# A state-space scan and a windowed attention in one kernel: output rows in pairs, last sums added on VectorE, K's weights in halves, another order of issue

## The chip, the cores and the metric

The kernel runs on one core of a Trainium2 chip. The metric is the device time of one execution in microseconds (us), the median of several runs. The engines named below are TensorE (PE; its weight loads are listed as PEld), VectorE (DVE), ScalarE (ACT), GpSimd (POOL) and SyncE (SP), which here does nothing but issue transfers; "SPq" is its queue. PSUM is the memory that TensorE writes its sums to; ScalarE and VectorE copy ("evict") them to SBUF, the core's working memory.

## The reference

There are two independent parts. Each takes its own input x of 2048 tokens by 448 values, in bf16. Their results are put side by side, 448 columns each, in one output of 2048 x 896.

```python
# Part A: state-space layer, 448 complex states
Lam_bar = exp(dt * Lam);  B_bar = ((Lam_bar - 1) / Lam)[:, None] * Bmat
Bu = einsum("bld,pd->blp", x, B_bar)
h[t] = Lam_bar * h[t-1] + Bu[t]                    # over 2048 tokens
y = 2 * real(einsum("blp,dp->bld", h, Cmat)) + x * Dskip
# Part B: attention of 16 heads of 28, each query sees the 8 keys s, s-2, .., s-14
q, k, v = split(x @ wqkv)
logits = einsum("bhsd,bhswd->bhsw", q, kg) * 28**-0.5   # kg, vg: the 8 keys and values of each query
attn = softmax(logits, masked where s - 2w < 0)
o = einsum("bhsw,bhswd->bhsd", attn, vg);  out = o @ wo
```

## The kernel before, in words

**Layout.** Token s = 16p + j stands in partition p (0 to 127) as token j (0 to 15). So what the text calls "token j" is 128 tokens of the sequence, one in each partition. Matrix products want the features on the partitions, so x is transposed: for tokens 12 to 15 by TensorE from a plain load (`pt_x`, L426), for the others by transposing DMAs (L361). 448 features are one block of 64 and three of 128; the block of 64 is handled by pairs of matmuls in the two halves of the array's rows (L483), the three others by L476.

**Part B.** The weights of K and then of Q are loaded by a helper `wload` (L338 for the three blocks of 128 features, L340 for the 64 that are left). Projections go to `qk_ps` (L476, L483, L509 for the last columns) and are evicted, some by ScalarE (L214, L216), some by VectorE (L218, L220; the line is a helper's). VectorE multiplies queries and keys (`prods`, L649 to L655), TensorE sums over the head's 28 values (L666), VectorE, ScalarE and TensorE make the softmax (L695 to L735). The values are evicted to `vd`; the rows that a partition needs from its neighbour are copied by DMA (the "halo", L775 and L776, four times). Then VectorE forms attention times values in four groups of four tokens, 3, 2, 1 and 0: per group four multiplications (L817) and the sums (L820). The windowed sum comes in two halves of 1792 columns, which for groups 3, 2 and 1 are added by L829; a transposing DMA (L857) and the `wo` matmuls (L885, L893) follow. In group 0, the last, nothing adds the halves: L832 adds the last product in two parts (tokens 0 and 1, then 2 and 3), and TensorE transposes by products with the identity (`pt_o`, L869), eight a token, two of which go to the same columns, so that PSUM adds the halves. ScalarE copies `pt_o` to SBUF (L874), four `wo` matmuls (L900) and an eviction (L214) follow. Token 2's eviction is shared by ScalarE (256 columns) and VectorE (192).

**Part A.** POOL prepares parameters, VectorE makes powers of Lam_bar (`pw`, L1182). For each of seven groups of states the input matmuls (L1232, L1241) fill PSUM, and a chain of matmuls and small ScalarE copies (L1256 to L1333) does the scan: within 16 tokens of a partition, then over the 128 partitions, and back. The carried state stands in a tile S of its own for the last token, so the step that hands the carry on takes a matmul of 128 columns and one of 384 (L1307, L1308). The output of a token is seven matmuls of 448 columns (L1434), with x * Dskip as further matmuls (L1430) or, for tokens 12 to 15, by VectorE (multiplied by L1411, added in the eviction by L1446).

**Outputs.** Each token's 448 columns of either part go out in one transfer of 128 x 448: L1449 for part A, L910 for part B, 32 in all. Staging rows come from rings: 8 rows for part A (`ya`), 4 for part B (`yb`). A row is taken at the eviction and is free again when its transfer has landed.

**Order.** All work is registered as units (an engine, a cost, predecessors, rings). Where the list `ORDER` has as many entries as there are units (687 before, 693 after), it is the order of issue as it stands; an entry above 1000 puts an eviction on the other of its two engines. Each engine works its list in order and waits at the head of it. Nearly all transfers are issued by SP, one after another, so a transfer whose data is not ready holds back all behind it. At the start TensorE runs products of zeros: `WARM` of them at once, and `FILL` of them behind each of the two batches of transposes.

Of the kernel before, what the change touches and what calls it, by code (L numbers as in the profile page):

```python
# [10 lines left out]
ALU = mybir.AluOpType  # L11
# [14 lines left out]
W = 8  # L26
# [6 lines left out]
QW = 2 + NCH  # L33
LV2 = ((1, 2, 3), (4, 8, 12), (16, 32, 48))
KPOW = sorted({1, 2, 4, 8, 12, 16} | {32 * k for ks in LV2 for k in ks})
# [4 lines left out]
WARM = 4  # L40
FILL = (1, 3)
# [4 lines left out]
YG = ((3,), (7,), (11,), (1, 5), (9,), (0, 4), (8,), (2, 6), (10,), (12, 13), (14,), (15,))  # L46
YSPLIT = 8
ORDER = [
# [156 lines left out]
class Ctx:  # L205
# [83 lines left out]
    def warm(self):  # L289
# [5 lines left out]
        nc.vector.memset(z, 0.0)  # L295
        box = {}
# [10 lines left out]
    def late_tile(self):  # L307
        if self.late is None:
            self.late = self.rc
            self.ya_v = self.late[:, 8448:8448 + 3584].rearrange("p (r d) -> p r d", r=8)  # L310
            self.yb_v = self.late[:, 12032:12032 + 1792].rearrange("p (r d) -> p r d", r=4)
            self.ya_ring, self.yb_ring, self.ya_row = Ring(8), Ring(4), {}
        return self.late


class PartB:
# [7 lines left out]
    def loads(self):  # L324
# [11 lines left out]
        def wload(c0, c1):  # L336
            w = self.wqk[:, :, c0:c1] if c0 < 2 * D else self.wv
            nc.sync.dma_start(w[:, 1:4], self.B_wqkv[DT:D, c0:c1].rearrange("(k p) c -> p k c", p=NCH))  # L338
            for rows in ((slice(DT, NCH),) if c0 < 2 * D else (slice(0, DT), slice(DT, NCH))):
                nc.sync.dma_start(w[rows, 0], self.B_wqkv[0:DT, c0:c1])  # L340
        self.wload = wload
# [4 lines left out]
        wload(D, 2 * D)  # L346
        self.u_x3 = [P.add("ACTQ", 0.0, lambda: None, lat=t) for t in (3.45, 3.95)]
        self.u_w["K"] = P.add("ACTQ", 0.0, lambda: None, lat=6.2)

    def loads_more(self):  # L350
# [16 lines left out]
        u0 = self.u0 = P.add("SP", 2.35, lambda: None, lat=0.0)  # L367
        self.u_w["Q"] = P.add("SP", 1.0, lambda: self.wload(0, D), [u0], -1, lat=4.4)
# [8 lines left out]
    def load_v(self, deps):  # L377
        self.u_w[2] = self.plan.add("SP", 1.2, lambda: self.wload(2 * D, 3 * D), deps, 0.5, lat=3.5)
# [32 lines left out]
    def prep(self, u_warm):  # L411
# [6 lines left out]
        def xpose(j):  # L418
            box = {}

            def tr():
                pt = box["pt"] = self.psum.tile([NCH, 2, KT, NCH], bf16, name="pt_x", tag="s")
                for n in range(2):
# [3 lines left out]
            u = P.add("PE", 0.9, tr, [self.u_x3[(j - 12) // 2]], -8.5, acq="s")  # L427
# [24 lines left out]
        def banks(b, r, tiles, boxes, prio, rfirst):  # L452
# [5 lines left out]
            for kind, kt in tiles:  # L458
                wd.append(self.u_wm if kind == "M" else self.u_w[kind])
# [1111 lines left out]
```

## Time and profile before

| what | value |
|---|---|
| device time, median of 3 runs | 139.18 us (138.98 to 139.67) |
| device time of the profiled execution | 140.44 us |
| its span from first to last instruction | 138.7 us |
| busy: PE, DVE, ACT, POOL | 131.6, 123.8, 90.0, 17.7 us |
| matmuls; instructions of DVE, ACT | 1078; 136, 202 |
| DMA | 39582 packets, 16.05 MB |
| output transfers | 32 of 112 KB, median 1.8 us from issue to landing |

Between the span and the device time of the profiled execution lie 1.7 us, and the profiled execution is 1.3 us above the median. A row of the groups reads: line, engine, operation, what it writes and reads with sizes, count | busy us, mean ns of one | idle time of the engine just ahead of these instructions and what ended it. In the timeline a row is: start, length, engine, line, operation, and in brackets the idle time ahead and what ended it. A row of the windows names a stretch of the span and then its length, the busy time and count of PE, PEld, DVE, ACT and POOL, the granted clock of TensorE, the share of the DMA engines that is busy and GB/s.

### The profile page before, as it was taken

What the parts mean: (1) busy time and instruction counts of PE and PEld (TensorE: products, weight loads), DVE (VectorE), ACT (ScalarE), POOL (GpSimd) and SP (SyncE); (2) the same over time, 40 slices, a digit from 0 to 9 for tenths busy, and PEclk for the clock granted to TensorE, in tenths of its full rate; (3) what the DMA queues carried; (4) which work ended last, traced back from release to release, by engine and by line L of the source; (5) the groups of instructions that cost most, each with busy time, mean ns of one, the idle gap of its engine ahead of it and who ended that gap; (6) DMA issues with size and microseconds to landing.
All of it is one profiled execution on the core that took longest, in us unless ns stands there. A gap on an engine that the chain in (4) does not pass through costs nothing.

```text
span 138.7 us, 2854 instructions
## 1 busy us (share of the span) xinstructions
PE 131.6 (95%) x1078; PEld 68.5 (49%) x1085; DVE 123.8 (89%) x136; ACT 90.0 (65%) x202; POOL 17.7 (13%) x69
## 2 busy tenths in 40 slices
PE   5999999999999999999999999999999999988990
PEld 1634435444555554756435564545655554534640
DVE  2268999899999999999999999999999999999820
ACT  3464589997563967776685998987637070722671
POOL 7489820028000000000000000000000000000000
PEclk9999999999999999999999999999999999999999
DMA  4979943645653349735898019000000827965774
GB/s 128 266 128 213 173 87 63 160 101 116 80 111 74 82 84 145 140 81 150 230 185 195 0 25 112 0 0 2 5 0 0 183 82 43 213 211 155 234 233 139
DMA packets 39582, 16.05 MB, mean 116 GB/s; under 512 B 31573, under 2 KB 38932, under 8 KB 39569
## 3 DMA queue, kind: packets, MB, share of 16 engines
q1 hardware_dynamic: 39506, 15.87, 54.0%
q8 instruction: 8, 0.13, 0.4%
q14 instruction: 5, 0.04, 0.1%
q10 hardware_dynamic: 63, 0.01, 0.0%
HBM read 4.32 MB, written 3.67 MB: 58 GB/s over the span
## 4 chain that ended last, share of the span: by engine, by line
DVE 35%; PE 31%; SPq 15%; issue 7%; DMA 6%; ACT 3%; DVEq 0%; ACTq 0%
DVE rb L820 13%; DVE prods L817 11%; SPq L361 8%; PE v_ps L762 7%; DVE rb L817 4%; PE qk_ps L476 4%; DMA out_dram<-qk 3%; PE logits L666 3%; PE y_ps L1434 3%; DMA rb<-in_B_x_dram 3%; DVE pw L1182 2%; DVE rb L829 2%; PE wo_ps L900 2%; PE scb L1232 2%; PE scp L1232 2%
## 5 line engine op out<-in xcount | busy, mean ns | idle before, releaser
L817 DVE TENSOR_TENSOR prods<-attn,vd 128x3584 bf16<-128x3584 bf16 x12 | 24.1, 2019 | 0.0
L820 DVE TENSOR_TENSOR rb<-rb,prods 128x3584 bf16<-128x3584 bf16 x11 | 22.2, 2021 | 0.1
L651 DVE TENSOR_TENSOR prods<-qk 128x3072 bf16<-128x3072 bf16 (+1 forms) x15 | 19.1, 1327 | 0.0
L214 ACT CAST qk<-wo_ps 128x448 bf16<-128x448 f32 (+1 forms) x16 | 8.3, 527 | 12.2 <-PE wo_ps L893 7.7
L1434 PE MATMUL y_ps<-Ccat,qk 128*128 128x448 bf16 x60 | 15.1, 352 | 0.1
L476 PE MATMUL qk_ps<-rb 128*128 128x512 bf16 x60 | 14.4, 379 | 0.0
L1434 PE MATMUL y_ps<-Ccat,h 128*128 128x448 bf16 x45 | 11.0, 352 | 0.9 <-ACT qk L214 0.9
L214 ACT CAST vd<-v_ps 128x448 bf16<-128x448 f32 x15 | 7.4, 539 | 5.8 <-PE v_ps L762 4.5
L1232 PE MATMUL scb<-xaT_sb,Bcat 128*128 128x512 bf16 x42 | 10.9, 380 | 0.0
L1232 PEld LDWEIGHTS <-Bcat 128*128 128x128 bf16 x84 | 7.6, 100 | 6.6 <-issue 0.4
L1284 ACT CAST ubuf<-scb 128x64 bf16<-128x64 f32 x35 | 7.1, 218 | 5.6 <-PE scb L1291 3.5
L762 PE MATMUL v_ps<-rb 128*128 128x448 bf16 x48 | 9.9, 353 | 0.0
L655 DVE TENSOR_TENSOR prods<-qk 128x768 bf16<-128x768 bf16 (+3 forms) x18 | 9.1, 569 | 0.3 <-ACT qk L214 0.2
L216 ACT ACTIVATE qk<-qk_ps 64x512 bf16<-64x512 f32 (+1 forms) x15 | 8.9, 599 | 0.6 <-PE qk_ps L509 0.3
L476 PEld LDWEIGHTS <-rb 128*128 128x128 bf16 x60 | 5.6, 98 | 7.1 <-DMA rb<-in_B_wqkv_dram 0.5
L1434 PEld LDWEIGHTS <-qk 128*128 128x128 bf16 x60 | 5.9, 98 | 5.3
L817 DVE TENSOR_TENSOR rb<-attn,vd 128x3584 bf16<-128x3584 bf16 x4 | 8.1, 2022 | 0.1
L893 PE MATMUL wo_ps<-wo_p,rb 128*128 128x448 bf16 x36 | 8.1, 354 | 0.0
L1182 DVE TENSOR_TENSOR pw<-Dm,spair 128x1920 bf16<-128x1920 bf16 x7 | 8.1, 1153 | 0.0
L214 ACT CAST qk<-qk_ps 128x512 bf16<-128x512 f32 (+2 forms) x11 | 6.3, 585 | 2.6 <-PE qk_ps L483 1.1
L1232 PE MATMUL scp<-xaT_sb,Bcat 128*128 128x512 bf16 x30 | 7.8, 380 | 0.0
L666 PE MATMUL logits<-prods,Zsel 128*32 128x256 bf16 x192 | 7.4, 274 | 0.0
(199 smaller groups left out, 261.9 us busy)
## 6 DMA issues: line engine op xcount, KB each, us to landing
out_dram<-qk SPq DMA_DIRECT2D x32, 112.0 KB, 1.8
vd<-vd SPq DMA_DIRECT2D x3, 392.0 KB, 4.7
rb<-in_B_wqkv_dram SPq DMA_DIRECT2D x3, 336.0 KB, 5.0
qk<-in_A_x_dram SPq DMA_DIRECT2D x1, 448.0 KB
ra<-in_A_B_re_dram SPq DMA_DIRECT2D x1, 392.0 KB, 4.3
ra<-in_A_B_im_dram SPq DMA_DIRECT2D x1, 392.0 KB, 5.9
rb<-in_A_C_re_dram SPq DMA_DIRECT2D x4, 98.0 KB, 2.9
rb<-in_A_C_im_dram SPq DMA_DIRECT2D x4, 98.0 KB, 2.8
```

The lines of the kernel that those rows point to most:

```text
L214: nc.scalar.copy(out, in_)
L361: nc.sync.dma_start(self.xT[:, j], bass.AP(x.tensor, x.offset + j * D - DT, [[T * D, NCH], [1, KT * NCH]]), transpose=True)
L476: nc.tensor.matmul(out(n), lhsT=w(n, full, k), rhs=self.xT[:, j:j + 4, k, :], start=(not rfirst and k == 1), stop=(rfirst and k == KT - 1) ...
L651: V.tensor_tensor(out.rearrange("p i j k q -> p i (j k) q"), qq.unsqueeze(1).to_broadcast([NCH, 2, 4 * nk, NCH]), bass.AP(kk.tensor, kk.of ...
L655: V.tensor_tensor(jk(out[:, i, a:e]), qq, kk, op=ALU.mult)
L666: nc.tensor.matmul(lg[32 * i:32 * i + 32, 2 * tp:2 * tp + 2, :], lhsT=cx.Z[:, kt, zs], rhs=pr[:, :, i, kt, :], start=(new and kt == 0), st ...
L762: nc.tensor.matmul(box["ps"][:].rearrange("p h d -> p (h d)"), lhsT=self.xT[:, j, k, :], rhs=self.wv[:, k, :], start=False, stop=(k == KT ...
L817: V.tensor_tensor(tmp[i].rearrange("p (j d h) -> p j d h", j=8, d=DH), aa, self.vd[:, o:o + 8], op=ALU.mult)
L820: V.tensor_tensor(acc, acc, tmp[i], op=ALU.add)
L1182: V.tensor_tensor(t[:], self.o["Dm"][:].rearrange("p (a b) -> p a b", b=2).unsqueeze(1).to_broadcast([NCH, 2 * NPW, 32, 2]), self.sp[:, m ...
L1232: mt(box[i], lhsT=self.Bcat[:, k, m, :], rhs=self.xk(slice(i, None, 4), k), start=(i % 2 == 0 and k == 0), stop=False, **kw)
L1434: nc.tensor.matmul(ps, lhsT=h, rhs=self.Ccat[:, m, :], start=(m == 0 and not skip), stop=(m == NM - 1), skip_group_check=True)
```

## The change

Line numbers here are those of the kernel after, unless said otherwise.

- **Output pairs.** Part A's 16 tokens leave in 8 transfers of 128 x 2 x 448 (L1492, the list `OUTP`), groups 3, 2 and 1 of part B in 6 (L939); the four tokens of group 0 still go one by one (L942). The ring `yb` has 6 rows. Rows are taken two at a time by units of their own, and freed together. Token 2's last eviction is one instruction.
- **Last sums.** With `MERGE`, VectorE adds the two halves of group 0 behind each of its two last additions (L855, 128 x 896), and `pt_o` takes four products a token in place of eight.
- **K's weights in halves.** K's columns come as 256 and 192 (L346). The 64 rows that are left, for K and Q, are one transfer that ScalarE issues. K's first projections (tokens 12 to 15) run as halves of two tokens; the copy of the 64 rows for the second half of the array is made per 128 columns. Tokens 14 and 15 have transposes and copies of their own.
- **Zero products.** `WARM` 4 to 5, `FILL` (1, 3) to (1, 2): the sum is eight in both.
- **Scan.** The tile S is gone; the states of the last block lie with gaps of four columns, so that the carry is one matmul of 512 columns (two places a group, 14 matmuls fewer, as many columns).
- **Order.** `ORDER` is another list. On TensorE, the seven output matmuls of one token of part A move behind the first eight `pt_o` products at the end. On SP, the second transpose of attention sums stands ahead of the last halo copy (L796, L797). On VectorE there is one eviction of `qk_ps` more (15 for 14), two copies of 64 x 512 more and one eviction to `vd` fewer.

```diff
-WARM = 4
-FILL = (1, 3)
+MERGE = 1
+WARM = 5
+FILL = (1, 2)
+OUTP = ((1, 5), (2, 6), (0, 4), (12, 13), (7, 11), (8, 9), (3, 10), (14, 15))
 ORDER = [
...
-        wload(D, 2 * D)
+        for c0, c1 in ((D, D + 256), (D + 256, 2 * D)):
+            nc.sync.dma_start(self.wqk[:, 1:4, c0:c1], self.B_wqkv[DT:D, c0:c1].rearrange("(k p) c -> p k c", p=NCH))
...
+        nc.scalar.dma_start(self.wqk[DT:NCH, 0], self.B_wqkv[0:DT, 0:2 * D])
+        nc.scalar.copy(cx.first[:, 1:2], cx.first[:, 0:1])
...
+            elif j == 12 and tiles[0][0] == "K":
+                us = []
+                for a in (0, 2):
+                    for n in range(2):
+                        us.append(P.add("PE", pe(3, 256), lambda n=n, a=a: f(n, a, a + 2), x[a:a + 2] + wd + us[-1:], prio, acq=None if a else "s"))
+                u = P.add("PE", pe(1, 512), rr, [us[-1]] + dup, prio, mode="r")
...
                         a, t = (v.rearrange("p (y j c) -> p y j c", y=2, j=4)[:, :, 2 * part:2 * part + 2] for v in (acc, tmp[3]))
                         V.tensor_tensor(a, a, t, op=ALU.add)
+                        if MERGE:
+                            V.tensor_tensor(a[:, 0], a[:, 0], a[:, 1], op=ALU.add)
...
-                    for y in range(2):
+                    for y in range(2 - MERGE):
                         c = y * n1 + a + kt * NCH
                         nc.tensor.matmul(pt[:, kt, :], lhsT=self.rb2[:, c:c + NCH], rhs=cx.ident[:],
-                                         start=(kt == 0 and y == 0), stop=(y == 1), skip_group_check=True)
+                                         start=(kt == 0 and y == 0), stop=(y == 1 - MERGE), skip_group_check=True)
...
-            def out(j=j, jb=jb):
-                nc.sync.dma_start(self.out_b[:, j, :], cx.yb_v[:, jb["y"]])
+            def out(j=j, jb=jb, g=g):
+                if g:
+                    a, b = jb["mate"]["y"], jb["y"]
+                    nc.sync.dma_start(self.out_b[:, j - 1:j + 1, :], cx.yb_v[:, a:b + 1:b - a])
+                    cx.yb_ring.put(a)
...
-            if j == 2:
-                es = [P.add("ACT", act(D - 192), lambda f=ev2: f(c1=D - 192), [u], pr, acq="yb")]
-                es.append(P.add("DVE", vec(192), lambda f=ev2: f(c0=D - 192, eng="DVE"), [u, *es], pr, rel="s"))
...
-            def carry(out, lt, Sc, hv):
-                mt(out[:, 0:NCH], lhsT=lt, rhs=Sc, start=False, stop=True, **kw)
-                mt(out[:, NCH:512], lhsT=lt, rhs=hv[:, 3, 0:384], start=False, stop=True, **kw)
...
+            def s6(box=box, L=L, hget=hget):
+                mt(box[0].rearrange("p (g c) -> p g c", g=4), lhsT=L(1), rhs=hget()[1][:, :, 2:2 + NCH],
+                   start=False, stop=True, **kw)
...
-            def out(j):
-                nc.sync.dma_start(self.out_a[:, j, :], cx.ya_v[:, cx.ya_row[j]])
-                cx.ya_ring.put(cx.ya_row[j])
+            def out(a, b):
+                nc.sync.dma_start(self.out_a[:, a:b + 1:b - a, :], cx.ya_v[:, rows[a]:rows[b] + 1:rows[b] - rows[a]])
+                cx.ya_ring.put(rows[a])
+                cx.ya_ring.put(rows[b])
```

More of the change, by code (lines that the diff above doesn't have):

```diff
@@ L295, in warm @@
         nc.vector.memset(z, 0.0)
+        self.first = self.pool.tile([NCH, 2], f32, name="first")
+        nc.vector.memset(self.first[:, 0:1], 0.0)
         box = {}
@@ L377, in load_v, with go @@
     def load_v(self, deps):
-        self.u_w[2] = self.plan.add("SP", 1.2, lambda: self.wload(2 * D, 3 * D), deps, 0.5, lat=3.5)
+        nc = self.nc
+        def go():
+            v = self.B_wqkv[:, 2 * D:3 * D]
+            nc.sync.dma_start(self.wv[:, 1:4], v[DT:D].rearrange("(k p) c -> p k c", p=NCH))
+            for rows in (slice(0, DT), slice(DT, NCH)):
+                nc.sync.dma_start(self.wv[rows, 0], v[0:DT])
+        self.u_w[2] = self.plan.add("SP", 1.2, go, deps, 0.5, lat=3.5)
     def alloc(self):
@@ L416, in prep, with xpose @@
         sc = DH ** -0.5
-        def xpose(j):
+        def xpose(j, nt):
             box = {}
             def tr():
-                pt = box["pt"] = self.psum.tile([NCH, 2, KT, NCH], bf16, name="pt_x", tag="s")
-                for n in range(2):
+                pt = box["pt"] = self.psum.tile([NCH, nt, KT, NCH], bf16, name="pt_x", tag="s")
+                for n in range(nt):
                     for k in range(KT):
@@ L470, in w, with f @@
                 return self.wm[rows, k].rearrange("p a c -> p (a c)") if kind == "M" else self.wqk[rows, k, c0:c0 + NCH]
-            def f(n):
-                if not rfirst:
+            def f(n, a=0, e=4):
+                if not rfirst and a == 0:
                     ps(n)
                 for k in range(1, KT):
-                    nc.tensor.matmul(out(n), lhsT=w(n, full, k), rhs=self.xT[:, j:j + 4, k, :],
-                                     start=(not rfirst and k == 1), stop=(rfirst and k == KT - 1), skip_group_check=True)
+                    nc.tensor.matmul(out(n)[:, a:e], lhsT=w(n, full, k), rhs=self.xT[:, j + a:j + e, k, :],
+                                     start=(not rfirst and k == 1 and a == 0), stop=(rfirst and k == KT - 1), skip_group_check=True)
             def rr():
@@ L1193, in scan, with pad @@
         mt = nc.tensor.matmul
[L1194 to L1195 removed]
+        h_out = [pool.tile([NCH, HW], bf16, name="h%d" % m) for m in range(NHO)]
         ubufs = [pool.tile([NCH, 2, PL], bf16, name="ubuf%d" % i) for i in range(NF)]
[L1197 removed]
+        def pad(ts):
+            for t in ts:
+                nc.gpsimd.memset(t[:, 1538:1539], 0.0)
+        u_pads = [P.add("POOL", 0.3, lambda: pad([t[:] for t in h_out]), [cx.boot], 1),
+                  P.add("POOL", 0.3, lambda: pad([cx.late_tile()[:, HW * i:HW * (i + 1)] for i in range(NM - NHO)]), qk_done, 1)]
         self.h = {}
@@ L1416, in outputs, with get @@
         nc, pool, P, cx = self.nc, self.pool, self.plan, self.cx
+        mate, rows, us_e, outs = {}, {}, {}, {}
+        for a, b in OUTP:
+            mate[a] = mate[b] = (a, b)
+            def get(a=a, b=b):
+                cx.late_tile()
+                rows[a], rows[b] = sorted(cx.ya_ring.get() for _ in range(2))
+            us_e[a, b] = [P.add("ACTQ", 0.0, get, self.u_h[4][:1], prio, acq=("ya", "ya"), lat=0.0)]
         for n, js in enumerate(YG):
@@ L1437, in ev @@
             def ev(eng, js=js, jb=jb):
-                cx.late_tile()
-                r = sorted(cx.ya_ring.get() for _ in js)
-                cx.ya_row.update(zip(js, r))
+                r = [rows[j] for j in js]
                 step = r[-1] - r[0] or 1
```

180 lines of the change are left out of this document (95 added, 85 removed), and 62 rows, old and new, of the table ORDER.

## The prediction

> **What bounds the kernel now.** I read the page's shares and slices first, then the windows, then the timeline from the last sums to the end.
>
> ```profile
> span 138.7 us, 2854 instructions
> PE 131.6 (95%) x1078; PEld 68.5 (49%) x1085; DVE 123.8 (89%) x136; ACT 90.0 (65%) x202; POOL 17.7 (13%) x69
> ...
> PE   5999999999999999999999999999999999988990
> ...
> DVE  2268999899999999999999999999999999999820
> ...
> DVE 35%; PE 31%; SPq 15%; issue 7%; DMA 6%; ACT 3%; DVEq 0%; ACTq 0%
> ```
>
> PE has the larger share, but from the fourth slice on DVE is as full. The windows put a number on it:
>
> ```profile
> core 0: us, PE busy (x) PEld busy (x) DVE busy (x) ACT busy (x) POOL busy (x), PEclk, DMA share, GB/s
> 9.84:128.62 118.78, 117.18 (x986) 60.84 (x992) 116.67 (x109) 79.81 (x186) 11.22 (x26) 1.00 0.51 103
> 128.60:135.80 7.20, 6.37 (x56) 3.84 (x53) 3.53 (x6) 5.41 (x11) 0.00 (x0) 1.00 0.74 237
> 135.80:138.70 2.90, 0.00 (x0) 0.00 (x0) 0.00 (x0) 0.00 (x0) 0.00 (x0) 1.00 0.38 120
> ```
>
> From its first eviction (9.84) to its last sum (128.62) DVE idles 118.78 - 116.67 = 2.11 us, PE 1.60. So both queues are full, and the end is the end of the last sum plus 138.7 - 128.62 = 10.1 us of tail. In that tail:
>
> ```profile
> 126.52 2.10 DVE L832 TENSOR_TENSOR rb<-rb,prods 128x1792 bf16<-128x1792 bf16 x2
> 128.50 1.49 PE L1434 MATMUL y_ps<-Ccat,S 128*128 128x448 bf16 x7
> 129.82 1.50 PE L869 MATMUL pt_o<-ident,rb 128*128 128x128 bf16 x24
> 132.27 0.61 PE L869 MATMUL pt_o<-ident,rb 128*128 128x128 bf16 x8
> 132.72 2.43 PE L900 MATMUL wo_ps<-wo_p,rb 128*128 128x448 bf16 x12
> 135.19 0.53 ACT L214 CAST qk<-wo_ps 128x448 bf16<-128x448 f32 x1 [0.22 <-PE wo_ps L900]
> 135.01 1.38 SPq L910 DMA_DIRECT2D out_dram<-qk  x3
> ```
>
> TensorE reaches `pt_o` only at 129.82, 1.2 us after the last sum: seven output matmuls stand ahead. So PE is slightly later than DVE, and a gain on one alone is worth at most that. Before this, PE itself was stopped once:
>
> ```profile
> 120.24 5.35 SPq L1449 DMA_DIRECT2D out_dram<-qk  x2
> ...
> 125.28 0.73 PE L1434 MATMUL y_ps<-Ccat,h 128*128 128x448 bf16 x3 [0.89 <-ACT qk L214]
> ...
> 127.55 0.53 ACT L214 CAST qk<-wo_ps 128x448 bf16<-128x448 f32 x1 [2.31 <-DMA out_dram<-qk]
> ```
>
> Two output issues took SP 5.35 us, ACT waited 2.31 for a staging row to come free, PE 0.89 for ACT.
>
> **The change part by part: VectorE up to its last sum.**
>
> ```profile
> L218 DVE CAST qk<-qk_ps 128x512 bf16<-128x512 f32 x5 | 3.3, 685 | 0.4 <-PE qk_ps L483 0.4
> L218 DVE COPY rb<-rb 64x512 bf16<-64x512 bf16 x2 | 0.6, 292 | 0.1
> L218 DVE CAST vd<-v_ps 128x448 bf16<-128x448 f32 x1 | 0.6, 614 | 0.0
> L1130 DVE TENSOR_TENSOR Gd<-Dm,gs 128x896 bf16<-128x896 bf16 x1 | 0.6, 621 | 0.0
> L1411 DVE TENSOR_TENSOR qk<-qk,rb 128x1792 bf16<-128x1792 bf16 x1 | 1.1, 1084 | 0.0
> L1446 DVE TENSOR_TENSOR qk<-y_ps,qk 128x448 bf16<-128x448 f32 x2 | 1.2, 620 | 0.5 <-PE y_ps L1434 0.5
> L1446 DVE TENSOR_TENSOR qk<-y_ps,qk 128x896 bf16<-128x896 f32 x1 | 1.1, 1081 | 0.0
> ```
>
> More work: one eviction of `qk_ps` (0.69), two copies of 64x512 (2 x 0.29 = 0.58), and two additions of 128x896 priced by the addition of the same size in L1130 (2 x 0.62 = 1.24; each needs the result just ahead of it). Less: one `vd` eviction (0.61). Sum +1.9 us. (The 192 columns of token 2's eviction lie behind the last sum.)
>
> The head sets where DVE's full stretch begins:
>
> ```profile
> 2.85 0.58 SPq L338 DMA_DIRECT2D rb<-in_B_wqkv_dram  x1
> ...
> 8.07 0.29 DVE L218 COPY wm<-rb 128x512 bf16<-128x512 bf16 x1 [0.82 <-DMA rb<-in_B_wqkv_dram]
> ...
> 9.84 0.68 DVE L220 TENSOR_SCALAR qk<-qk_ps 128x512 bf16<-128x512 f32 x1
> ...
> 10.87 0.69 DVE L218 CAST qk<-qk_ps 128x512 bf16<-128x512 f32 x1 [0.35 <-PE qk_ps L483]
> ```
>
> ```profile
> L476 PE MATMUL qk_ps<-rb 128*128 128x512 bf16 x60 | 14.4, 379 | 0.0
> ```
>
> Q's weights, issued at 2.85, are there at about 8.0, when the copy that waits for them starts. The halves of K let K's matmuls start sooner, but the next work of PE needs Q, and Q's transfer is still the fifth on SP (three for K become two of other sizes, the 64 rows go to ScalarE's queue). I take it to land at 7.5 to 7.9. Between it and VectorE's first eviction TensorE's list has work worth 7.5 matmuls of 512 columns, 1.8 us at 14.4 / 60 = 0.24, and three pairs of the 64-row block at about one matmul each, 0.7. The eviction then starts at 10.0 to 10.4, and I take 10.3: a loss of 0.46. If Q lands as late as before, it is 10.6 (a loss of 0.8); if Q lands 0.8 sooner than before, 9.8 (none). The zero products, eight both times, cost and bring nothing.
>
> Idle time: of the 2.11 us, 0.9 are three waits, the rest gaps between dependent operations:
>
> ```profile
> DVE qk L218 <- PE qk_ps L483: 0.4, 1, 0.4
> DVE prods L649 <- ACT qk L214: 0.3, 1, 0.3
> DVE prods L655 <- ACT qk L214: 0.2, 1, 0.2
> ```
>
> All three lie before 31 us and are shorter than the 0.46 by which DVE starts later plus its added copies, so I let most of them go: 1.35 us remain (bounds: 0.9 and, with new waits in an order that I can't time, 3). The new end of the last sums, the second L855, is 10.3 + 116.67 + 1.9 + 1.35 = 130.2, that is 1.6 later than 128.62.
>
> **TensorE.** `pt_o` loses 16 products: by 1.50 us for 24 and 0.61 for 8 about 0.06 each, some 1 us, of which half follows the last sum. Merged carries and halved K matmuls keep their columns; I cost them at nothing (bounds: 14 instructions of some 0.05 less; six more of as much more), hidden by DVE. The output matmuls of one token (1.3 us from 128.50 to 129.82) move behind the first `pt_o`, and with pairs the 0.89 stop should go: it came from the row ring behind the third transposing DMA, where six single outputs and two loads are now three pairs and one load. PE is then free for `pt_o` at 129.82 - 1.31 - 0.89 = 127.6; tokens 0 and 1 are ready at 130.2 - 1.08 - 0.62 = 128.5. Slack 0.9 us: with the stall still there it is just used up, and any more goes to the end one for one.
>
> **The tail.** Behind 130.2 DVE has xd (1.08), the eviction of the pair 12, 13 (1.08) and of 14 and 15 (0.62 each): 3.25 us with their overlaps. SP then has the pair (14, 15) and three single rows. By 1.38 us for three issues they follow at 0.47, so the last one starts 3.35 + 3 x 0.47 = 4.75 us after the last sum. PE's side, four products (0.25), ACT's copy of 128x512 (0.59), two tokens' `wo` matmuls (2 x 0.8), an eviction (0.53) and the waits between them, ends 4.25 after it, inside this. The last issue before began at 135.95 (third of the row at 135.01), 2.75 ahead of the end. So the tail is 4.75 + 2.7 = 7.45 in place of 10.1: -2.65.
>
> **Transfers.** The output issues before the tail fall from 28 to 14 by 0.45: SP is not the limit but for its waits. Pairs give up something: a row of the first token waits for the second, and both stay taken until the landing. Six rows for four in `yb` cover that for B; for A eight rows remain.
>
> **Sum.** 130.2 + 7.45 = 137.65 against 138.7: -1.05 us. The profiled execution took 140.44, 1.7 around its span and 1.26 above the median; I apply the difference to the median: 139.18 - 1.05 = 138.1.
>
> A rule of the Trainium skill speaks against a step. "DMA: Bandwidth & Descriptors", Specifications, gives 512 B as the smallest transfer for line rate and says that below it the engine reads, changes and writes. K's second half has runs of 384 B (192 columns of two bytes), where before each run had 896 B. If that makes Q land an estimated 0.4 us later, the sum by the rule is -0.65 rather than -1.05. No run here shows it yet: before, no run of these weights is that short.
>
> **The rivals.**
>
> (a) *No measurable difference* (within 0.5%, 0.7 us, about what a measurement of this kernel tells from no change). DVE's idle stays at 2.1 or a little more and Q lands no earlier: 130.2 + 0.75 + 0.3 = 131.2, end 138.7, 139.2 us. For it: both queues are full, so there is no room for 1.9 us of more work. Against: 2.65 us off the tail rest on rows. In it the change's head does not do what it says.
>
> (b) *Slower*: the outputs in pairs hold their rows behind the third transposing DMA. Place: part A's evictions at about 120 to 128.
>
> ```profile
> 114.81 1.52 SPq L857 DMA_TRANSPOSE rb<-rb  x1
> ```
>
> ```profile
> L910 SPq DMA_DIRECT2D out_dram<-qk x16: 388/435/1388, 109.5 to 136.0; - x16
> ...
> DMA to landing us min/median/max: 1.7/1.8/4.6
> ```
>
> An output usually lands after 1.8 us, one behind the transpose after 4.6. If a pair must wait for its second token and then lands that late, ACT waits 2.31 more, as at 127.55, while PE needs its eviction, and PE stops for 0.89 + 2.31 = 3.2 us; less the slack of 0.9 that is 2.3 over the forecast, 140.4. It makes the kernel slower from a stop of 0.9 + 1.05 + 0.7 = 2.65 on.
> A wait of DVE that could look like it, for the last halo, I hold for covered:
>
> ```profile
> L775 SPq DMA_DIRECT2D vd<-vd x4: 553/582/1164, 60.5 to 72.9; - x4
> ...
> DMA to landing us min/median/max: 2.6/4.7/4.7
> ```
>
> ```profile
> L817 DVE TENSOR_TENSOR prods<-attn,vd 128x3584 bf16<-128x3584 bf16 x12 | 24.1, 2019 | 0.0
> ```
>
> The halo copies now stand behind the second transposing DMA of sums: 1.5 for its issue, 0.6 for the copy's and up to 4.7 from there to the landing, 6.8, with the second copy's issue some 7.7, against 4 x 2.02 = 8.1 us of multiplications and additions that DVE has before it needs them.
>
> (c) *A larger gain*: Q lands near 7.2, DVE starts by 9.8 and idles 0.9 only: 129.3 + 7.45 = 136.7, 137.2 us.
>
> **How the numbers follow.** Forecast 0.57, (a) 0.18, (b) 0.16, (c) 0.09. The forecast's own range is 137.5 to 138.5 and (c) is on its side, so faster 0.65; a few of the forecast's cases end within 0.7 us of before, which (a) holds already: same 0.19, slower 0.16. The range goes from 136.9 (three quarters of (c)) to 139.9 (all of (a), the milder third of (b)), which leaves out some 0.13.
>
> **What would show it.** In the profile of the changed kernel: the first L223 eviction of `qk_ps` at 10.0 to 10.6; DVE's idle from there to the second L855 under 1.6 us; the second L855 ending at 130.2, two rows of 0.62 for it; `pt_o` of tokens 0 and 1 starting at once behind the first L855; no PE wait on ACT between 118 and 128; last output issue 4.75 us after the last sum, and 2.7 from there to the end. The prediction is wrong if DVE has waits that sum to over 2.5 us (halo, `attn`, `qk`), if PE reaches `pt_o` after 129, or if outputs land over 4 us after their issue with an engine waiting for the row.

## The result and the profile after

The changed kernel takes 141.39 us (median of 4 runs, 141.33 to 141.82) beside 139.43 for the kernel before; the ratio is 1.0149, 95% interval 1.0108 to 1.0189. A later comparison with more runs gives 141.41 beside 140.70, ratio 1.0052 (1.0026 to 1.0078). So it is slower, by 0.7 to 2.0 us, where 1.1 us less was forecast. The kernel after is steady between comparisons (141.39, 141.41); the kernel before is not: its medians lie between 139.4 and 140.7. As its executions spread over some 3 us, and a ratio leaves out those that lie over 1.5% above the fastest, a ratio sets a kernel of small spread against the lower part of that spread; so medians stand beside the ratios below.

The page of the kernel after:

```profile
span 139.7 us, 2803 instructions
PE 132.1 (95%) x1061; PEld 67.7 (48%) x1061; DVE 125.8 (90%) x141; ACT 89.3 (64%) x202; POOL 17.1 (12%) x75
...
DVE 73%; issue 9%; PE 8%; DMA 4%; SPq 3%; ACT 0%; DVEq 0%
```

Before, the chain that ended last was shared by DVE (35%) and PE (31%). Now 73% of it is DVE's: by this chain VectorE sets the time from some 12 us to the last sum. Windows of the kernel after, from the first eviction, and from the first product of queries and keys to the end of the last sum:

```profile
10.46:130.70 120.24, 118.08 (x980) 60.35 (x979) 118.25 (x111) 81.17 (x188) 9.58 (x30) 1.00 0.51 105
16.17:131.29 115.12, 112.42 (x955) 58.00 (x954) 113.32 (x103) 77.43 (x181) 4.60 (x15) 1.00 0.47 102
```

The same second window of the kernel before:

```profile
15.16:128.62 113.46, 111.86 (x960) 58.80 (x967) 111.82 (x100) 77.27 (x180) 6.50 (x13) 1.00 0.48 99
```

VectorE's last sum ends 131.29 - 128.62 = 2.67 us later: the first product starts 1.01 later (16.17 for 15.16), from there VectorE has 1.50 more work (113.32 for 111.82), and its idle time is 0.16 more (1.80 for 1.64). Behind the last sum come 139.70 - 131.29 = 8.41 us in place of 10.1. Together that is 1.0 us more, the difference of the two spans (139.7 and 138.7).

The timeline of the kernel after, VectorE and then TensorE:

```profile
64.86 1.22 DVE L717 TENSOR_REDUCE mx<-logits 128x128 bf16<-128x1024 f32 x1 [0.74 <-PE logits L288]
...
129.01 0.63 DVE L855 TENSOR_TENSOR rb<-rb 128x896 bf16<-128x896 bf16 x1
...
130.67 0.62 DVE L855 TENSOR_TENSOR rb<-rb 128x896 bf16<-128x896 bf16 x1
```

```profile
129.69 0.56 PE L892 MATMUL pt_o<-ident,rb 128*128 128x128 bf16 x7
131.35 0.23 PE L892 MATMUL pt_o<-ident,rb 128*128 128x128 bf16 x1 [1.10 <-DVE rb L855]
131.42 0.73 PE L1479 MATMUL y_ps<-Ccat,h 128*128 128x448 bf16 x3
131.99 0.92 PE L1479 MATMUL y_ps<-Ccat,qk 128*128 128x448 bf16 x4
132.74 0.39 PE L892 MATMUL pt_o<-ident,rb 128*128 128x128 bf16 x4
```

Here is the surprise. Of the eight identity products of tokens 0 and 1, seven run and the eighth waits 1.10 us for the second L855, the sum of tokens 2 and 3. A token has 448 columns, three and a half blocks of 128. The fourth product of a token reads 128 columns, and 64 of them belong to the next token; with the sums cut at column 896, the end of token 1, its last product needs the second part. The seven output matmuls that could have filled the wait stand behind it.

And TensorE's waits in the kernel after:

```profile
PE pt_o L892 <- DVE rb L855: 1.1, 1, 1.1
PE ps_b L1203 <- DVE qk L221: 0.7, 1, 0.7
PE pt_at L743 <- DVE attn_t L737: 0.5, 1, 0.5
PE logits L687 <- DVE prods L672: 0.3, 1, 0.3
```

All four are waits for VectorE. Before, the largest behind the head was the 0.9 for ScalarE at 125 us; that one is gone, as forecast, and four others have come.

### The profile page after: what moved, and what is told of

Same layout as the page of the kernel before. It is cut to its first block, busy times and chain, and to the rows that moved or that the text cites. A ratio compares the mean times of both kernels' runs of the same rounds, so it can differ in the third digit from the quotient of the medians.

```text
span 139.7 us, 2803 instructions
## 1 busy us (share of the span) xinstructions
PE 132.1 (95%) x1061; PEld 67.7 (48%) x1061; DVE 125.8 (90%) x141; ACT 89.3 (64%) x202; POOL 17.1 (12%) x75
## 4 chain that ended last, share of the span: by engine, by line
DVE 73%; issue 9%; PE 8%; DMA 4%; SPq 3%; ACT 0%; DVEq 0%
DVE rb L841 15%; DVE prods L838 14%; DVE prods L672 11%; DVE prods L676 6%; DVE rb L838 6%; DVE qk L221 4%; DVE pw L1221 3%; DVE prods L670 3%; SPq L362 3%; DVE rb L850 2%; PE wo_ps L923 2%; DMA rb<-in_B_x_dram 2%; PE qk_ps L489 2%; DMA ra<-in_B_x_dram 2%; DVE qk L223 2%
## 5 line engine op out<-in xcount | busy, mean ns | idle before, releaser
L1479 PE MATMUL y_ps<-Ccat,qk 128*128 128x448 bf16 x64 | 15.9, 352 | 0.0
L489 PE MATMUL qk_ps<-rb 128*128 128x512 bf16 (+1 forms) x66 | 15.1, 363 | 0.3 <-DMA rb<-in_B_wqkv_dram 0.3
L217 ACT CAST vd<-v_ps 128x448 bf16<-128x448 f32 x16 | 7.9, 541 | 6.5 <-PE v_ps L783 4.7
L1479 PE MATMUL y_ps<-Ccat,h 128*128 128x448 bf16 x48 | 11.7, 353 | 0.0
L217 ACT CAST qk<-wo_ps 128x448 bf16<-128x448 f32 x16 | 8.2, 538 | 4.7 <-PE wo_ps L916 4.0
L217 ACT CAST qk<-y_ps 128x448 bf16<-128x448 f32 (+1 forms) x9 | 5.5, 670 | 6.2 <-issue 4.0
L489 PEld LDWEIGHTS <-rb 128*128 128x128 bf16 x66 | 6.2, 99 | 6.8 <-DMA rb<-in_B_wqkv_dram 0.8
L219 ACT ACTIVATE qk<-qk_ps 64x512 bf16<-64x512 f32 (+1 forms) x14 | 8.0, 596 | 1.5 <-PE qk_ps L530 1.4
```

Source lines behind the costliest of these rows:

```text
L217: nc.scalar.copy(out, in_)
L219: nc.scalar.mul(out, in_, scale)
L489: nc.tensor.matmul(out(n)[:, a:e], lhsT=w(n, full, k), rhs=self.xT[:, j + a:j + e, k, :], start=(not rfirst and k == 1 and a == 0), stop=( ...
L1479: nc.tensor.matmul(ps, lhsT=h, rhs=self.Ccat[:, m, :], start=(m == 0 and not skip), stop=(m == NM - 1), skip_group_check=True)
```

## The experiments

Theory T: VectorE sets the time, and the eighth product adds 1.1 us in the tail. Rivals: R, the outputs in pairs; P, TensorE is the bound and VectorE follows; Q, the late weights set the head.

### How large is the loss?

The unchanged kernel after, in more runs:

> The kernel after once more, with more rounds beside the kernel before. If the first comparison (4 executions each, ratio 1.0149) caught the kernel before at its lower end: ratio 1.008 to 1.012, the 1.0 us by which the two profiles differ or a little more. If not: 1.013 to 1.017, and some 0.9 us stay unexplained. Its profile shows the wait of 1.1 at the identity product, 0.7 at the maximum and the first product of queries and keys at 16.0 to 16.8 again.

Measured 141.41 us beside 140.70, ratio 1.0052 (1.0026 to 1.0078). Its profile has the waits again (1.10 at the eighth product, 0.74 at the maximum) and the first product at 16.73. The loss is smaller than the first comparison said, and even below the expected range; it is the kernel before that stands at another level.

Most variants below were measured in other comparisons than the kernel after, and single edits with ratios of 1.0058 to 1.0074 can't be told from its 1.0052 by the ratio. What a single edit does is therefore read from its profile, with the median as a second sign.

### The last sums: where they are cut, and whether they are merged

```diff
-a, t = (v.rearrange("p (y j c) -> p y j c", y=2, j=4)[:, :, 2 * part:2 * part + 2] for v in (acc, tmp[3]))
+c0, c1 = ((0, 960), (960, 1792))[part]
+a, t = (v.rearrange("p (y c) -> p y c", y=2)[:, :, c0:c1] for v in (acc, tmp[3]))
```

> The kernel after, but the two last sums are cut at column 960 instead of 896, so that the first part holds the 64 columns of token 2 that the last identity product of token 1 reads as well. Theory T (in the changed kernel that product waits 1.1 us for the second part, and the seven output matmuls placed to cover the wait stand behind it): the wait of the product on the second L855 is gone, TensorE's last matmul and the end come 1.1 us sooner, 140.3 us. Rival R (the end is set by the outputs in pairs on SyncE's queue): within 0.3 us of 141.4. Rival V (VectorE alone sets it): no gain, since VectorE's sums take 0.03 us more.

Measured 140.91 us, ratio 1.0062 (1.0032 to 1.0091), span 138.9. TensorE's timeline in it:

```profile
129.52 0.62 PE L893 MATMUL pt_o<-ident,rb 128*128 128x128 bf16 x8 [0.18 <-DVE rb L856]
...
133.90 1.67 PE L924 MATMUL wo_ps<-wo_p,rb 128*128 128x448 bf16 x8 [0.48 <-DVE qk L1490]
```

All eight products run without a stop: the shared 64 columns were the cause. The gain of the median is 0.5 of the 1.1 us; 0.48 us comes back as a wait of a `wo` matmul for VectorE's evictions (L1490), which by the program give a PSUM buffer free.

Without the merge:

```diff
-MERGE = 1
+MERGE = 0
```

> The kernel after without the two additions of the halves (L855): eight identity products a token, as before. Theory T: the last sum ends 1.25 us sooner at about 130.05, TensorE has 16 products of 0.054 more (0.9), 8 of them ahead of the waiting product; it stops the wait of 1.1, so the end comes 0.3 to 0.6 sooner: 140.8 to 141.1. Were the merge a gain by itself: 0.5 or more later than after, 141.9. Rival R: within 0.3 of 141.4.

Measured 140.75 us, ratio 1.0061 (1.0033 to 1.009). The last sum ends at 129.76, 1.53 sooner; 0.26 of it is this execution's earlier first eviction (10.20), and the rest is about the 1.25 of the two additions. The sixteen products of the first two tokens run without a stop from 129.21, and the median is 0.64 to 0.66 us lower, just past the 0.3 to 0.6 of theory T. So in this kernel the merge costs more than it saves, by the profile and the medians; the ratio alone doesn't show it.

The merge alone in the kernel before:

```diff
                         V.tensor_tensor(a, a, t, op=ALU.add)
+                        V.tensor_tensor(a[:, 0], a[:, 0], a[:, 1], op=ALU.add)
...
-                    for y in range(2):
+                    for y in range(1):
...
-                                         start=(kt == 0 and y == 0), stop=(y == 1), skip_group_check=True)
+                                         start=(kt == 0 and y == 0), stop=True, skip_group_check=True)
```

> The kernel before with the merge alone: the two additions of the halves behind the two last sums, four identity products a token for eight. Theory T: the last sum ends 1.25 us later, at about 130, where TensorE arrives at 129.8 with all output matmuls of part A behind it, so nearly nothing is waited for (the product that reads token 2's columns waits 0.1 to 0.3); 16 products of 0.054 go, 0.5 to 0.8 us less: ratio to before 0.995 to 0.998. If VectorE's added work counts in full: 0.4 us more than before, 1.003.

Measured 140.15 us, the same median as the kernel before beside it (140.15), ratio 1.0054 (1.0022 to 1.0086): not the gain expected. The order there has token 1 first, and so it is the fourth product that waits:

```profile
129.42 0.33 PE L870 MATMUL pt_o<-ident,rb 128*128 128x128 bf16 x3
130.30 0.68 PE L870 MATMUL pt_o<-ident,rb 128*128 128x128 bf16 x9 [0.55 <-DVE rb L833]
```

Three run, then 0.55 us of waiting for the second sum. That the stop falls on the eighth product where token 1 is second and on the fourth where it is first is a second sign of the shared columns.

> The same with the cut at column 960. Theory T: 0.1 to 0.3 us less than with the cut at 896, ratio to before 0.994 to 0.997. If the shared columns played no part: the same as with the cut at 896.

Measured 140.23 us, ratio 1.0035 (0.9997 to 1.0072). The cut at 960 takes that stop away; behind it, the next token's products wait 0.18 us for ScalarE instead, and the `wo` matmul 0.55 for ScalarE's copy. The 0.1 to 0.3 us expected of the cut did not come, and the difference between the two is inside the intervals: the merge brings nothing in either.

### Is VectorE's work in the head the cause?

Two of VectorE's evictions go to ScalarE:

```diff
-    1063, 73, 1065, 12, 1059, 66,
+    63, 73, 1065, 12, 59, 66,
```

> The kernel after, but two of the evictions of 128x512 of K's projection that VectorE makes at about 12 to 15 us go to ScalarE, which has a gap there. Theory T: VectorE is the bound up to the last sum, so the second L855 ends 1.2 to 1.4 us sooner (at about 130.0); the product that waits for it then waits only some 0.1 us, and the end comes about 1.1 us sooner, 140.3. Rival R (outputs): no change. Rival P (TensorE is the bound and VectorE only follows): L855 sooner by less than 0.5, VectorE idle instead, no change in the end.

Measured 141.07 us, ratio 1.0074 (1.0042 to 1.0105). VectorE's timeline in it:

```profile
10.79 1.29 DVE L223 TENSOR_SCALAR qk<-qk_ps 128x512 bf16<-128x512 f32 x2 [2.39 <-PE qk_ps L496]
...
14.56 1.41 DVE L223 TENSOR_SCALAR qk<-qk_ps 128x512 bf16<-128x512 f32 x2 [0.83 <-PE qk_ps L530]
```

1.37 us of work left VectorE, and 0.83 of it came back as a wait for TensorE's next projection. The last sum ended at 131.16, 0.13 us sooner only; 0.33 us of the rest is this execution's later first eviction. In the head rival P holds: there VectorE follows TensorE.

### The head: what TensorE does first

K's second halves and its pairs go ahead of Q's matmuls, and VectorE takes one tile of K ahead of Q's (entries of the order):

```diff
-    40, 31, 30, 54, 7, 55, 48, 68, 45, 1049, 56, 69, 20, 57, 60, 58, 70, 61, 1072, 11, 62, 1071, 36, 32, 1050, 88, 1064,
-    13, 93, 1063, 73, 1065, 12, 1059, 66,
+    40, 1049, 31, 30, 54, 7, 48, 55, 56, 57, 68, 45, 69, 20, 70, 60, 61, 1059, 1072, 11, 62, 1071, 36, 58, 32, 1050, 88, 1064,
+    13, 93, 1063, 73, 1065, 12, 66,
```

> The kernel after with another order at the head alone: K's second halves and K's pairs of the 64-row block run ahead of the six matmuls of Q, and VectorE evicts K's first tile ahead of Q's (the copy of x that the pairs need goes ahead of a chain of small parameter operations). Theory H (VectorE's first product comes 1.0 us later than before because TensorE's list has Q's matmuls ahead of the end of K, and VectorE has no eviction to do meanwhile): the first eviction starts at 8.5 to 9.5 in place of 10.2 to 10.8, the first product of queries and keys (L670) at 15.0 to 15.5 in place of 16.2, the last sum 0.7 to 1.1 us sooner; the wait of 1.1 at the identity product goes with it, so the end is 0.7 to 1.0 sooner, 140.5. Rival Q (Q's weights land too late for anything to help): first product within 0.3 of 16.2, the end within 0.3 of 141.4.

Measured 140.71 us, ratio 1.0058 (1.0018 to 1.0098). VectorE's timeline in it:

```profile
8.40 0.69 DVE L220 CAST qk<-qk_ps 128x512 bf16<-128x512 f32 x1
10.03 1.29 DVE L222 TENSOR_SCALAR qk<-qk_ps 128x512 bf16<-128x512 f32 x2 [0.94 <-PE qk_ps L495]
...
15.46 1.22 DVE L669 TENSOR_TENSOR prods<-qk 128x1536 bf16<-128x1536 bf16 x1
```

The first eviction moves from 10.46 to 8.40 (it is K's now; Q's follows at 10.03), the first product from 16.17 to 15.46. The last sum moves from 131.29 to 130.75, less than the 0.7 to 1.1 expected, and the median is 0.7 lower. The wait of 1.10 at the eighth product is there unchanged, against the expectation. The first product differs between executions of one kernel: it starts at 15.96 to 16.73 in the five profiles with the head of after, at 15.41 to 15.87 in the three with K first, and at 14.73 to 15.73 in the eight with the head of before. Their means are 16.2, 15.6 and 15.2. So some 0.6 us of the lost 1.0 was the order of TensorE's list; the copy that waits for Q's weights starts at about the same times in both (7.55 to 8.20, and 7.48 to 7.74).

> Both: the head's order and the sums cut at column 960. Theory T with H: the two gains overlap, since TensorE then arrives at the identity products when they are ready; end 1.2 to 1.8 us ahead of after, 139.6 to 140.2, about the kernel before. If they add: 2 us. Rival Q: as the cut alone, 140.9.

Measured 140.17 us beside 140.41 for the kernel before, ratio 1.0003 (0.9971 to 1.0035); by the medians that is 1.2 us less than after, what the two gains (0.5 and 0.7) come to when added, so they don't overlap as theory T has it. This step is the best shown: in the same comparison the kernel after with its pairs undone, which behaves as after (below), has the ratio 1.011 (1.0075 to 1.0144). With two small edits the loss is gone.

K's weights in one transfer again:

```diff
-        for c0, c1 in ((D, D + 256), (D + 256, 2 * D)):
+        for c0, c1 in ((D, 2 * D),):
```

> The kernel after with K's 384 feature rows in one transfer of 448 columns in place of 256 and 192 (runs of 896 B in place of 512 and 384). If runs under 512 B cost as the Trainium skill's page DMA: Bandwidth & Descriptors says: Q's weights land 0.3 us or more sooner than in after (7.85) and the first eviction starts as much sooner, end 0.3 sooner. If they don't: Q within 0.2 us, K's first matmuls 0.3 us later behind the zero products, first eviction and end within 0.2 us.

Measured 141.82 us (4 runs, 141.48 to 143.14), ratio 1.0141 (1.0059 to 1.0223). K's first matmuls start at 6.54 in it and the first eviction at 10.95. In the five other profiles whose head is that of after, K's matmuls start at 5.88 to 6.25 and the first eviction at 10.16 to 10.82. So in this one profile the single transfer is 0.3 to 0.7 us later for K and brings no earlier eviction. Q's transfer is issued at 2.20 in place of 2.74, as it has one fewer ahead of it, and the copy that waits for Q starts at 7.56: 0.29 ahead of after, but inside the 7.55 to 8.20 of the five. So a cost of the short runs isn't seen here; a small one isn't excluded either. As to the time, 141.82 and 141.4 lie within the intervals.

### The wait at the maximum

The first multiplication of attention and values goes between the last product and the maximum, on top of the two edits (in the order, the subtraction of the maximum and the exponential move back a few places too):

```diff
         def top():
+            if b == 0:
+                self.early()
...
                     if n == 0:
-                        mul(0)
+                        if b == 0 or r == 0:
+                            mul(0)
                         mul(1)
+                    elif n == "first":
+                        mul(0)
...
+                if n == 0 and b == 1 and r == 1:
+                    self.early = lambda step=step: step("first")
```

> The head's order and the cut at column 960, and as a third edit the first multiplication of attention and values (2.02 us) set between the last product of queries and keys and the maximum that waits 0.74 us for TensorE's sums (the subtraction of the maximum and the exponential stand later in their lists to match). Theory M (that wait delays everything on VectorE behind it, to the end): no wait of VectorE above 0.3 us between 16 and 130, last sum 0.7 us sooner than with the two edits (130.35), end 0.4 to 0.8 sooner: 139.4 to 139.8, ratio to before 0.993 to 0.998. If TensorE is the bound by then: last sum sooner, the end within 0.2 of 140.2.

Measured 139.71 us (12 runs) beside 140.25 for the kernel before, ratio 0.9966 (0.9932 to 0.9999). VectorE's timeline in it:

```profile
61.76 1.75 DVE L671 TENSOR_TENSOR prods<-qk 128x3072 bf16<-128x3072 bf16 x1
63.43 2.02 DVE L839 TENSOR_TENSOR rb<-attn,vd 128x3584 bf16<-128x3584 bf16 x1
65.37 1.22 DVE L718 TENSOR_REDUCE mx<-logits 128x128 bf16<-128x1024 f32 x1
```

The wait of 0.74 is filled, the median falls by 0.46 from the version with two edits, and the last sum ends at 130.09 though this execution's first eviction (8.82) was 0.46 later than that one's. The two medians come from different comparisons, so the size of this step is less sure than that the wait is gone.

### The outputs: pairs and staging rows

Pairs undone in the kernel after (each pair sent as two transfers; part A's likewise, at L1492):

```diff
-                    nc.sync.dma_start(self.out_b[:, j - 1:j + 1, :], cx.yb_v[:, a:b + 1:b - a])
+                    nc.sync.dma_start(self.out_b[:, j - 1, :], cx.yb_v[:, a])
+                    nc.sync.dma_start(self.out_b[:, j, :], cx.yb_v[:, b])
```

> The kernel after with every pair sent as two transfers of one token, at the same place, rows still taken and freed in pairs. Theory T (SyncE has slack in this order, since the two tokens' evictions set when it can issue): within 0.3 us of after, 141.4. If the pairs bring something: 0.5 us or more later. Rival R (a pair lands later, 2.2 us for 1.8): 0.4 us sooner.

Measured 141.42 us, ratio 1.011 (1.0075 to 1.0144), between the two ratios of the kernel after itself (1.0149 and 1.0052): no difference by the median (141.39 and 141.41 for the kernel after). In this order SyncE has slack. The kernel before with six rows for `yb` (the rows of x behind them move up), and then with six rows and pairs:

```diff
-            self.yb_v = self.late[:, 12032:12032 + 1792].rearrange("p (r d) -> p r d", r=4)
-            self.ya_ring, self.yb_ring, self.ya_row = Ring(8), Ring(4), {}
+            self.yb_v = self.late[:, 12032:12032 + 2688].rearrange("p (r d) -> p r d", r=6)
+            self.ya_ring, self.yb_ring, self.ya_row = Ring(8), Ring(6), {}
```

> The kernel before with six staging rows for part B in place of four. Theory T: ScalarE no longer waits for a landed output near 127.5, TensorE's stop of 0.6 to 0.9 us near 125.5 goes, TensorE reaches the identity products 0.6 to 0.9 us sooner, at about the time of the last sum: ratio to before 0.994 to 0.996. If the stop is by something else (the PSUM buffers, the matmuls ahead): the stop stays, ratio 1.0.

> As the last one, and outputs two tokens a transfer (part A in 8, groups 3 to 1 of part B in 6, each issued where the second token of the pair was issued). Theory T: SyncE has slack, so within 0.3 us of the kernel with six rows alone. Rival R (pairs hold rows and land late, 2.2 us for 1.8): a wait of ScalarE for landed outputs comes back and the time is 0.5 us or more above the kernel with six rows.

Six rows: 139.45 us beside 140.15, ratio 0.9988 (0.9955 to 1.0021), not the 0.994 to 0.996 expected. With pairs: 140.66, ratio 1.0065 (1.0034 to 1.0096); all nine of its runs (140.43 to 140.77) lie above all ten of the other's (138.78 to 140.13). In the old order the pairs cost 1.2 us. The profile with pairs, SyncE, ScalarE and TensorE, and the same eviction with six rows alone:

```profile
119.47 6.74 SPq L1472 DMA_DIRECT2D out_dram<-qk  x2
...
124.90 0.91 ACT L215 CAST qk<-y_ps 128x896 bf16<-128x896 f32 x1 [3.13 <-DMA out_dram<-qk]
...
125.86 0.73 PE L1448 MATMUL y_ps<-Ccat,h 128*128 128x448 bf16 x3 [1.16 <-ACT qk L215]
```

```profile
123.26 0.91 ACT L214 CAST qk<-y_ps 128x896 bf16<-128x896 f32 x1 [1.75 <-DMA out_dram<-qk]
```

SyncE's row spans two issues of under 0.5 us each, at 119.47 and 125.83, and the time between them, in which it waits for ScalarE. ScalarE waits 3.13 us for two rows of part A that are free only when a whole pair has landed, and TensorE 1.16 for ScalarE. With six rows alone the same eviction waits 1.75 and TensorE doesn't stop. This is the rival on rows held by pairs, at its place, in the kernel before. In the kernel after, with another order, no output takes over 2.4 us to land, and the stop is not there.

Six rows in the kernel before, with more runs, and the kernel before profiled twice more:

> The kernel before with six staging rows once more, with more rounds, beside the last one on the same chip. If the stop of TensorE at 125 that the profiles of before show (0.64 and 0.89) is in most of its executions: 0.5 us or more under before, ratio 0.996 or less. If most of them don't have it: ratio 0.998 to 1.001.

> The kernel before once more, for a second profile of it, since its first profiled execution was 1.26 us above its median. Theory T: the shape is the same: VectorE's last sum at 127.5 to 128.6, TensorE with no or a shorter stop at 125, and a tail of 9 to 10 us; span 137.5 to 138.7. If the first profile was typical: 138.7 with the stop of 0.9 again.

> The kernel before, a third profile. If the stop near 125 hangs on how late single outputs land, it differs from 0.64 and 0.89, and the execution's time with it; if it belongs to every execution, it lies between 0.6 and 0.9 again and the time near 140.5.

Six rows: 139.61 us beside 140.25, ratio 0.9959 (0.9926 to 0.9991), and no stop of TensorE at 125 in either profile. The two further profiles of before have spans of 139.0 and 139.5 (executions of 140.75 and 141.2), above the 137.5 to 138.7 expected, and the stop at 0.6 both times, so it belongs to its usual executions. The slower one's waits of TensorE:

```profile
PE y_ps L1434 <- ACT qk L214: 0.6, 1, 0.6
PE scb L1241 <- DMA xaT_sb<-in_A_x_dram: 0.5, 1, 0.5
PE qk_ps L476 <- DMA rb<-in_B_x_dram: 0.5, 1, 0.5
```

The last two, for transposed inputs, are not in the other two profiles: how late they land differs between executions of one kernel. That the longer time of this execution comes from them is likely but not shown, and why a whole comparison stands higher than another stays open.

In the one comparison that has both, the kernel before with six rows (139.61) and the kernel after with its three edits (139.71) are 0.3% to 0.4% below the kernel before (140.25), and they do not differ from each other. The other comparison of six rows (0.9988) shows no gain clear of noise. The scan's single carry, the zero products and the rest of the new order were not undone one by one, so what they bring or cost isn't shown.

## Why the prediction was wrong

**What bounds the kernel: right.** Both engines full, the end at the last sum plus a tail.

**VectorE's work: nearly right.** From the first eviction to the end of the last sum it is 118.84 (118.25 in the window to 130.70 and 0.59 of the last L855) for a forecast of 116.67 + 1.9 = 118.57. The additions of the halves took 0.63 and 0.62 as priced. The 0.27 too much are no added work: the first product of queries and keys took 1.34 us where the same product took 0.96 before, while GpSimd ran beside it (last section).

**The head: right by its own marker, which was the wrong one to watch.** The first eviction came at 10.46 for a forecast of 10.3. The first product came 1.01 later. Of that, 0.62 is the later first eviction; the other 0.39 is what VectorE does between the two, 0.68 more work and 0.29 less idle time. K first on TensorE brings back some 0.6 of the 1.0. I had noted that order as work worth 7.5 matmuls without asking whether VectorE had anything to do meanwhile. K came in two transfers before, not three, so Q's is the fifth on SP both times. The rule on transfers below 512 B, from the Trainium skill's "DMA: Bandwidth & Descriptors", Specifications, is not seen to matter: with runs of 896 B again the copy that waits for Q started inside the spread of the others, and the first eviction came no sooner (10.95). One run of four executions doesn't decide more than that.

**Idle time: wrong.** 1.99 us for a forecast of 1.35. The waits I named did go; another came, 0.74 at the maximum. Before, one of the `pw` products (L1182) stood between the last product and the reduction that needs TensorE's sum of it, and in the new order nothing does. The kernel before:

```profile
60.58 1.76 DVE L651 TENSOR_TENSOR prods<-qk 128x3072 bf16<-128x3072 bf16 x1
62.25 1.16 DVE L1182 TENSOR_TENSOR pw<-Dm,spair 128x1920 bf16<-128x1920 bf16 x1
63.37 1.22 DVE L695 TENSOR_REDUCE mx<-logits 128x128 bf16<-128x1024 f32 x1
```

The kernel with three edits, which fills the place again, has no such wait.

**TensorE free at 127.6, slack 0.9: wrong, but without cost.** Its weight loads for the identity products stood waiting for 0.52 us until the first L855 had ended at 129.64, so TensorE was there at 129.17, and the first seven products ran at 129.69. It was 1.6 later than forecast: waits for VectorE of 0.72, 0.49 and 0.30 came, and a head that ends later. I had treated the delays of VectorE as if TensorE did not see them before the end. As the sums were 1.1 later too, TensorE still came first. The stop of 0.89 went, as said, but not by the pairs that I named: in the kernel before, six rows alone remove it, and pairs bring it back as 1.16. As the reason was wrong, it is luck that this step came true.

My reading of SyncE ahead of that stop was wrong too. The row of 5.35 us holds two issues, of 0.46 at 120.24 and of 0.33 at 125.26; between them SyncE waited for ScalarE's eviction.

**The tail of 7.45: wrong, 8.41, and the step that failed most.** The step by which TensorE's side ends 4.25 after the last sum, inside this tail, counts four identity products behind the last sum and none of the seven output matmuls, as these were to fill the time from 128.5 on. By the shared columns the eighth product waited for the second L855 as well, so the step that tokens 0 and 1 are ready at 128.5 (129.64 by the first L855) held for seven of eight products only, and the seven output matmuls (1.3 us) came behind the last sum. In the kernel after:

```profile
133.94 2.43 PE L923 MATMUL wo_ps<-wo_p,rb 128*128 128x448 bf16 x12
...
136.41 0.53 ACT L217 CAST qk<-wo_ps 128x448 bf16<-128x448 f32 x1 [0.22 <-PE wo_ps L923]
...
135.46 1.85 SPq L942 DMA_DIRECT2D out_dram<-qk  x3
```

The last eviction ends at 136.94, 5.65 us after the last sum at 131.29 in place of 4.25, and the last output issue follows it instead of coming at 4.75 by SyncE's count. From there to the end it is 2.8 as forecast (2.7). Taken by itself the merge was then a cost, as VectorE pays 1.25 ahead of the last sum, and TensorE's saving lies behind a wait. In sum the misses are 0.16 for the head, 0.27 for work, 0.64 for idle time and 0.96 for the tail: 2.0 us, from 137.65 to 139.70.

**From the span to the median: wrong by up to 1.3.** I took the profiled execution for 1.26 above the kernel's level, from three runs. More runs put the median of before between 139.4 and 140.7, so that execution was ordinary. The forecast for the changed kernel, 137.65 of span and 1.7 around it, would have been 139.4 by itself.

**The rivals.** The one that forecast a slower kernel had the right sign by luck, as the time was lost at another place: not one wait of ScalarE for a landed output lies behind 118 us in the kernel after. Its mechanism is real, though, as the kernel before with pairs shows.

## What to carry to other kernels

When the work on one engine is cut in parts so that another can start early, check which bytes the first consumer reads and not only which item it is for: a block of 128 over items of 448 columns reaches into the next item. Where two engines are both full, a later one delays the other all along the way, so follow each wait between them instead of adding the work of each. And take the level of a kernel from as many runs as the difference you forecast needs.

## What the runs showed of the hardware

Where a product on VectorE and a pair of products on GpSimd ran at once, one or both took longer. GpSimd and VectorE at about 16 us in the kernel after:

```profile
15.62 1.08 POOL L1161 TENSOR_TENSOR spair<-ex,cs 128x210 bf16<-128x210 f32 x2
...
16.17 1.34 DVE L670 TENSOR_TENSOR prods<-qk 128x1536 bf16<-128x1536 bf16 x1
```

and the same two in the kernel with three edits:

```profile
15.40 1.83 POOL L1168 TENSOR_TENSOR spair<-ex,cs 128x210 bf16<-128x210 f32 x2
...
15.87 0.96 DVE L669 TENSOR_TENSOR prods<-qk 128x1536 bf16<-128x1536 bf16 x1
```

The product took 1.34 us beside GpSimd's 1.08, or 0.96 beside its 1.83. With two evictions moved to ScalarE both did, 1.36 beside 1.79. The other products of this size in the kernel after took 0.94 to 0.96, and GpSimd's pair took 1.08 in the kernel before, where no such product runs beside it. No run here was made to find the cause.

Two tokens in one output took 2.2 us from issue to landing, one token 1.7. In the kernel after:

```profile
out_dram<-qk SPq DMA_DIRECT2D x14, 224.0 KB, 2.2
...
out_dram<-qk SPq DMA_DIRECT2D x4, 112.0 KB, 1.7
```
